# Pairs of chunks in halves, u by one product, one more chunk transposed by DMA, and another order of all steps

## The chip, the cores and the metric

The kernel runs on one core of a Trainium2 chip. The metric is the device time of one execution in microseconds. Engines, as the profile names them: PE (TensorE matmul; PEld is its weight load), DVE (VectorE), ACT (ScalarE), POOL (GpSimd) and SP (SyncE), whose queue issues nearly all DMAs here.

## The reference

Two parts, the second on the result of the first. B = 4, H = 8, S = 768, D = 48; the second part has 3072 tokens, 384 inputs and 2048 inner columns.

```python
    for t in range(S):
        kt, vt, rt, wt = (k[:, :, t].copy(), v[:, :, t].copy(), r[:, :, t].copy(), w[:, :, t].copy())
        cur = np.einsum('bhd,bhe->bhde', u[None] * kt, vt)
        y[:, :, t] = np.einsum('bhd,bhde->bhe', rt, state + cur)
        state = wt[:, :, :, None] * state + np.einsum('bhd,bhe->bhde', kt, vt)
...
    h = x @ w_in
    g = np.maximum(0.01 * h, h)
    return (g @ w_out).astype(np.float32)
```

`x` is `y` with the heads side by side, one row a token.

## The kernel before, in words

The sequence of every batch entry is cut into chunks of 128 tokens: 4 entries of 6 chunks, 24 chunks with the numbers n = 0 to 23 in the order of `seq`. For a chunk the recurrence becomes matrix products. The logarithm of w is summed over the tokens by a product with a triangular matrix (cum); exponentials of the sums scale r and k (the rk products on DVE); r and k are transposed (tr by PE and a copy, or trk/trk2 by a DMA transpose); scores are k against r, masked on DVE; intra multiplies the masked scores with v and adds what the state gives; the state goes on to the next chunk of the entry. What u adds is taken separately: ru and ruk on POOL, a sum over a head (dg) on DVE, vs on POOL. The result y of a chunk is transposed into `xT`, by PE and a copy (ty, ty_copy) or by a DMA (ty_dma, ty_dma2).

The first four chunks are two pairs (`pair`, lines 390 to 599): a pair loads 256 tokens of an entry at once, two tokens to a partition, j = 0 and 1. `PARTS` (line 64) cuts the first pair into two halves of four heads; the second runs whole. `HALVES` (line 65) names the tensors that are loaded in halves where there are parts. A part has three cum products (banks c1, c0, cg) and four exponentials, one each for k and r and for j = 0 and 1, and four rk products, four transposes and four copies. The other 20 chunks go by `single` (lines 604 to 751); `run` (753 to 788) joins the chunks in `MERGED` with the next one, and `RK_DMA` (line 61) says whose r and k a DMA transposes, `Y_DMA` whose y.

The second part works on blocks of one or two chunks (`BLOCKS`, line 69). An up step (up2 for two chunks) is six products of `w_in_b` with `xT` into one PSUM bank (line 846); ACT applies the leaky function into `g` (line 858); a down step is four products of `g` with `w_out_b` (line 871), four of them to a chunk; the result is copied into one of 24 `o` buffers (line 877) and stored (line 830). The weights come in ten pieces as float32 (line 299) and are cast to bfloat16 by DVE, ACT or POOL.

The order of all work is written out as `TABLE` (lines 73 to 123): each word is an engine's letter (P, V, A, G for POOL, S for SP) and the number of a step in the order in which `step` was called; `Z512` is a product of zeros with 512 columns, which keeps PE at work while there is nothing else. `HOMES` says which buffer of its pool each tile takes. `issue` (lines 40 to 58) calls the steps in that order, so each engine's own order is that of its words, and an engine waits at an instruction whose input is not there, with all its later ones behind it. The pools are small: 7 `in` buffers for loads, 8 PSUM banks, 24 `o` buffers. Line 231 is the helper of all element-wise products, 235, 237 and 239 the copies on POOL, DVE and ACT, 242 the helper of all products; 353 and 384 are PE's transposes.

The vector u must lie on all partitions (`ub`). Before, its one row is split into three bfloat16 parts of decreasing size by two subtractions on DVE, and three products with a single row of ones (lines 336 to 339) add them up on 128 partitions; DVE copies the sum out.

Of the kernel before, what the change touches and what calls it, by code (L numbers as in the profile page):

```python
# [8 lines left out]
BF16 = mybir.dt.bfloat16  # L9
# [15 lines left out]
class Steps:  # L25
# [51 lines left out]
P94 V72 G57 S145 P93 A102 P95 G65 V49 A99 P96 S91 P73 A101 G56 P81 A98 V75 A97 P76 A100 G154 P77 V74 P79 S151
V106 P66 S156 G121 P78 V103 P107 A82 V67 P104 G117 P83 V108 A105 P80 P68 V112 A84 V85 G155 P113 A69 V109 A114
P86 V148 A87 P110 G118 S149 A111 P740 S159 A146 G122 P129 V119 P132 V131 A741 P732 S162 G116 V134 P730 G120 A733
V123 P738 G115 A731 V130 G124 A152 P125 V133 P136 A739 V126 S165 P138 P135 S171 P137 P127 A158 V157 P736 S168  # L80
V139 A128 P742 S173 V142 A737 P140 V150 P744 A743 A141 P143 P734 A745 V144 P758 V161 G160 A735 P768 A759 P760
A769 P752 A761 V163 P746 A164 S252 P770 P762 A771 P766 V167 A763 G166 S201 P764 A175 A767 P177 P772 S172 A765
V178 P753 A179 S200 A773 P754 A180 V169 G170 P747 S231 V181 P748 A256 P183 S174 P749 V184 G216 P258 S202 V750
P755 A260 A261 V259 P774 G187 A756 S253 V182 A263 P775 A262 G188 P185 A204 S757 P780 V186 S229 V189 P206 P191
S203 V207 P776 V193 A208 G176 P777 S295 A209 V192 G190 P194 P781 A778 V211 G217 A195 V210 P196 P214 S254 P782
V197 A215 G270 V265 P198 P212 V218 S232 A199 P783 A213 P268 A233 P790 S230 V269 A784 P220 A791 G205 P235 S785
V222 P788 G219 A238 A237 S356 V236 P223 P786 A789 G297 S327 V221 G251 A224 P792 A787 V264 S292 G274 P225 A239
P266 A793 P794 V226 G234 A240 V241 P227 G271 P795 V267 S779 A228 V242 P243 S255 P804 G247 V272 A244 S324 P245
A805 P278 G248 P802 V246 S293 V279 P275 A803 G358 V249 P796 G329 V284 G250 P797 S294 V276 A296 P806 V285 A798
S353 P298 V277 A807 P800 G257 V299 S799 P280 G273 A801 P286 S326 P288 V281 A303 P808 S376 V287 A328 A302 V289  # L90
P282 P330 G310 A300 P809 V305 S355 A283 A332 V331 A301 P290 P308 G311 A291 P810 V304 A335 V309 S436 P822 G314
A334 V312 A333 P306 A357 P824 G313 S325 A823 P359 A307 G343 V336 P318 P826 S378 A362 V319 A361 A825 G375 P315
V360 A380 P811 S354 V317 A364 P382 A827 V316 P828 S377 A385 A812 V383 P820 A829 G449 P320 S419 A386 P814 A821
V321 G339 A363 P816 V337 S416 A815 V365 P347 A387 G340 P322 V388 P818 S338 A817 V348 A384 P390 A819 P367 G398
V366 P830 A368 V391 S437 G371 V341 P402 P369 P831 V389 S473 A370 G342 V403 P392 P832 V323 A393 G372 P846 S751
A420 P399 G421 V373 A847 S435 G394 P422 V408 S418 P842 A425 A424 V401 G434 P344 A843 P833 S813 V423 G374 S417
V346 P848 A427 A834 G450 V400 P844 A849 S492 V409 P404 A426 G395 P850 A845 V451 S835 V405 P836 S471 V396 A439
P406 V345 P837 A407 S491 V428 P441 P349 A443 P838 V442 S633 V350 A444 P851 A445 G453 V429 A446 P351 V447 P839
G430 S438 V352 P458 V448 P858 A840 V459 G431 S454 P862 A859 P860 A475 V432 A863 P477 G433 P856 A861 V478 S841
G504 P864 A479 S490 A857 P866 A482 G646 A865 P872 A867 G505 P870 A480 A481 S545 P873 G440 A871 V506 S379 G489  # L100
P874 V483 P466 G452 P455 S524 V467 P852 V457 S472 P853 V465 P868 A494 V464 S543 A854 P496 V456 A869 P468 P878
V497 S474 V469 A499 P460 A501 G381 P879 S470 A500 V461 G397 A498 P410 V503 P412 A528 V411 P462 P880 S544 A463
V413 G508 P530 V484 S581 P414 P875 A533 V502 G485 A415 S493 V531 P881 A876 G486 A535 P888 V882 S877 A532 A534
P884 G476 S509 V487 A889 G542 P898 A885 P513 A547 G488 P916 V514 A899 P549 G557 A917 S883 P890 V550 S526 P894
G558 A552 A553 P912 A891 V555 G495 A895 V559 P896 G507 A551 A554 P519 S525 P886 A913 G561 V556 S598 A897 P892
V520 A887 P510 S546 A893 P900 V512 P920 S599 V517 P914 V518 S601 P901 V536 A915 V511 G538 P521 S579 P902 V537
G539 V522 A602 P515 S562 P903 V516 G560 P604 V540 A904 P918 V605 G548 P906 A607 G612 A919 S523 P574 A608 P907
V575 A609 G603 P908 A606 V611 G616 P909 A583 P627 P585 V910 P921 S905 A588 V628 A587 S580 G597 P922 V586 S600
P923 A589 A590 S527 V591 P563 V924 P938 V564 S925 P934 V572 A939 S634 P936 V573 A935 S683 P926 V565 A937 G593
S855 V592 P576 A927 P940 S632 V577 G594 P928 V610 A941 S578 G613 P932 V595 A929 P930 A933 G529 V614 S617 P948  # L110
G541 A931 P566 P568 G647 V567 P942 V569 G615 P943 S911 V648 S582 P570 P944 A571 A636 P945 P638 A946 P968 V639
S947 P958 A641 A969 S651 P956 A642 S652 A959 V644 P618 S654 A957 P964 V626 A640 A643 G650 P960 V620 A965 S653
P954 G584 V645 A961 G596 V619 P962 S681 A955 V625 P621 P623 A963 V622 P976 S700 A655 V624 P629 G665 P657 S701
V630 P977 A659 A660 V658 G669 P978 S631 A662 P966 G656 A661 V664 G666 P949 V663 A967 P950 A685 S670 V667 P951
G668 A704 P687 P979 A952 V688 P706 G714 A689 S953 P970 A691 V707 S635 A980 P992 V693 A692 A711 P984 A993 V713
P986 A690 S981 A985 G699 P982 S703 A709 A987 P971 S682 A708 A983 G718 S702 P671 A710 P972 V672 P973 S684 V673
G637 P988 V676 A974 G649 P674 V677 S975 A989 P990 V675 G705 P678 A991 P996 V679 G695 P994 V694 S680 A997 P998
G696 V712 A995 P999 G715 V697 P1000 S719 P1001 G686 V716 G698 P1004 A1002 G717 P1005 S1003 P1016 P1024 A1017
P1012 A1025 P1014 A1013 P1010 A1015 P1020 A1011 P720 A1021 P1026 V721 P1018 V722 P1006 V725 A1019 P723 V726
P1027 V724 P727 P1007 V728 P1022 S729 A1008 P1028 A1023 P1032 P1033 S1009 P1034 P1035 P1029 A1036 P1046 S1037  # L120
V1030 P1050 S1031 A1047 P1040 A1051 P1042 A1041 P1044 A1043 P1038 A1045 P1048 A1039 P1052 A1049 P1060 A1053
P1054 P1055 P1056 P1057 P1061 A1058 P1062 S1059 P1063 A1064 S1065
"""
HOMES = (
    "011210004235675110025210037100001114300041341020240167253225224320212025111271366401653130562140410444310107"
    "444272305601001212120043005177140225601220401051021114200353274511022260670313331121036313301196100440121742"
    "504220870120064100260413210122710123450512147342005013010101002312517222025412461372403310044031120141615210"
    "020122604062612005060072121072217511121234633241173402213183112102134400002021020524174643000102607102234261"
    "9510011101604132200034052000102211712121223536200045025736374120325140253603166271113648046455256290a114706b"
    "0735102751c5d1336653223e4f041115g1357257360h1i0572622253k6j1016020610l4m075127623107n12604375151320"  # L130
# [4 lines left out]
def kernel(  # L135
# [58 lines left out]
    ones_f = pool.tile([1, 128], BF16, name="ones_f")  # L194
# [97 lines left out]
    def weights(which, lo, hi):  # L292
# [697 lines left out]
```

## Time and profile before

| what | before |
|---|---|
| median of 3 runs | 182.56 us |
| lowest, highest | 180.97, 182.56 us |
| the profiled execution | 181.88 us |
| its span in the profile | 180.1 us |
| PE busy, instructions | 171.3 us (95%), 1960 |
| ACT, DVE, POOL busy | 118.6, 112.2, 101.3 us |
| DMA | 34.60 MB, mean 192 GB/s |

The span goes from the first instruction of the program to the last; some 1.8 us of the execution's own time lie around it. A busy PE is not PE at its peak, since its products are pipelined and overlap: the pace is read from the starts of successive ones. The DMA share is the mean busy share of the 16 DMA engines and can exceed 1, as transfers on one engine overlap.

### The profile page before, as it was taken

The page shows a single profiled execution, that of the slowest core. Times are in us where ns is not written, and L with a number is a line of the kernel's source. Part 1 is how long each engine was busy: PE and PEld are TensorE (multiplying, and loading weights), DVE is VectorE, ACT ScalarE, POOL GpSimd, SP SyncE. Part 2 cuts the span into 40 slices and gives each one's busy share as a digit, 9 for nine tenths or more (in the row PEclk, how much of TensorE's full clock was granted, in tenths as well). Part 3 has the DMA queues.
Part 4 walks back from the last instruction along what each step waited for, and adds up shares of the span by engine and source line. Part 5 has one row for each costly group of instructions (what it writes and reads, how often), then busy time and mean ns, then how long its engine had stood idle before and what let it go on. Part 6 is the DMA issues. An engine that isn't in the chain of part 4 may idle for free.

```text
span 180.1 us, 5012 instructions
## 1 busy us (share of the span) xinstructions
PE 171.3 (95%) x1960; PEld 128.1 (71%) x1960; DVE 112.2 (62%) x230; ACT 118.6 (66%) x265; POOL 101.3 (56%) x137
## 2 busy tenths in 40 slices
PE   7978899999999999999999999989999999999992
PEld 2645688766878787778777977577786786876860
DVE  7489882459688879796398587686396384070000
ACT  3676987855966898667757954555776953722821
POOL 6799722467695858947946928567068378000000
PEclk9999999999999999999999999999999999999999
DMA  5999999799998989989999999999899998403202
GB/s 147 265 315 297 346 375 333 177 202 221 177 224 159 227 156 204 231 197 195 206 186 146 244 192 165 197 218 223 201 185 169 191 216 103 126 2 91 87 0 87
DMA packets 117129, 34.60 MB, mean 192 GB/s; under 512 B 109681, under 2 KB 116338, under 8 KB 117106
## 3 DMA queue, kind: packets, MB, share of 16 engines
q1 hardware_dynamic: 117104, 34.28, 91.6%
q8 instruction: 15, 0.25, 0.6%
q14 instruction: 8, 0.07, 0.2%
q10 hardware_dynamic: 2, 0.00, 0.0%
HBM read 25.17 MB, written 4.72 MB: 166 GB/s over the span
## 4 chain that ended last, share of the span: by engine, by line
PE 61%; DMA 12%; ACT 7%; POOL 6%; DVE 5%; issue 5%; SPq 2%; POOLq 0%; DVEq 0%; ACTq 0%
PE ps L242 59%; DMA in<-in_w_dram 6%; DMA in<-in_r_dram 3%; POOL ru L231 3%; DMA xT<-y 2%; DVE rk L231 2%; DVE m L231 2%; ACT g L858 2%; PE ps L353 1%; SPq L618 1%; ACT ps L651 1%; POOL sb L231 1%; POOL vs L231 1%; ACT lw L626 1%; POOL vb L235 1%
## 5 line engine op out<-in xcount | busy, mean ns | idle before, releaser
L242 PE MATMUL ps<-xT,w_in_b 128*128 128x256 bf16 (+1 forms) x672 | 70.6, 257 | 0.9 <-DMA xT<-y 0.6
L242 PE MATMUL ps<-w_out_b,g 128*128 128x384 bf16 x384 | 71.4, 326 | 0.0
L858 ACT ACTIVATE g<-ps 128x512 bf16<-128x512 f32 x96 | 56.4, 597 | 14.5 <-PE ps L242 12.3
L242 PEld LDWEIGHTS <-w_in_b 128*128 128x128 bf16 x672 | 57.1, 98 | 8.8 <-issue 0.8
L242 PEld LDWEIGHTS <-g 128*128 128x128 bf16 x384 | 34.7, 97 | 18.9
L231 DVE TENSOR_TENSOR m<-ps,maskb 128x512 bf16<-128x512 f32 x40 | 25.3, 683 | 9.9 <-PE ps L242 9.6
L231 DVE TENSOR_TENSOR rk<-ps,in 128x384 bf16<-128x384 f32 (+1 forms) x52 | 26.2, 520 | 7.9 <-ACT ps L651 2.6
L231 POOL TENSOR_TENSOR ru<-in,ub 128x384 f32<-128x384 f32 x24 | 23.8, 1001 | 11.5 <-DMA in<-in_k_dram 11.2
L231 POOL TENSOR_TENSOR sb<-s,a 128x384 bf16<-128x384 f32 x18 | 14.9, 830 | 17.3 <-ACT a L647 13.9
L231 POOL TENSOR_TENSOR ru<-ru,in 128x384 f32<-128x384 f32 x24 | 23.8, 1001 | 0.8
L239 ACT COPY o<-ps 128x384 f32<-128x384 f32 x19 | 9.1, 480 | 16.1 <-PE ps L242 16.0
L231 POOL TENSOR_TENSOR vs<-in,dg 128x384 f32<-128x384 f32 x20 | 16.5, 830 | 1.6 <-DVE dg L367 1.6
L235 POOL CAST vb<-in 128x384 bf16<-128x384 f32 x24 | 12.0, 504 | 8.4 <-DMA in<-in_v_dram 8.4
L367 DVE TENSOR_REDUCE dg<-ru 128x8 f32<-128x384 f32 x24 | 13.1, 547 | 5.3 <-POOL ru L231 5.1
L231 DVE TENSOR_TENSOR ci<-ps,lw 128x384 f32<-128x384 f32 x20 | 11.1, 555 | 6.6 <-PE ps L242 3.6
L231 DVE TENSOR_TENSOR y<-ps,vs 128x384 bf16<-128x384 f32 x20 | 11.1, 553 | 4.2 <-PE ps L242 4.2
L242 PEld LDWEIGHTS <-rkT 48*128 48x128 bf16 (+2 forms) x304 | 10.6, 97 | 3.5 <-issue 1.7
L626 ACT ACTIVATE lw<-in 128x384 bf16<-128x384 f32 x20 | 10.3, 521 | 3.1 <-DMA in<-in_w_dram 3.1
L647 ACT ACTIVATE a<-ps 64x4 f32<-64x4 f32 x36 | 6.1, 169 | 8.3 <-PE ps L242 4.2
L651 ACT ACTIVATE ps<-ps 128x384 f32<-128x384 f32 x20 | 9.6, 481 | 2.3 <-DVE ci L231 2.0
L654 ACT ACTIVATE ps<-ci 128x384 f32<-128x384 f32 x20 | 9.8, 496 | 0.9 <-DVE ci L231 0.9
L353 PE MATMUL ps<-ident,rk 128*128 128x128 bf16 x88 | 9.0, 227 | 1.4 <-DVE rk L231 1.2
(75 smaller groups left out, 164.3 us busy)
## 6 DMA issues: line engine op xcount, KB each, us to landing
out_dram<-o SPq DMA_DIRECT2D x24, 192.0 KB, 3.4
in<-in_r_dram SPq DMA_DIRECT2D x22, 192.0 KB, 4.3
in<-in_w_dram SPq DMA_DIRECT2D x22, 192.0 KB, 4.1
in<-in_k_dram SPq DMA_DIRECT2D x22, 192.0 KB, 4.3
in<-in_v_dram SPq DMA_DIRECT2D x20, 192.0 KB, 4.3
in<-in_moe_w_out_dram SPq DMA_DIRECT2D x4, 768.0 KB, 10.4
in<-in_moe_w_in_dram SPq DMA_DIRECT2D x2, 768.0 KB, 7.0
in<-in_moe_w_in_dram SPq DMA_DIRECT2D x4, 384.0 KB, 7.5
```

Of the source, the lines that this page charges most:

```text
L231: (nc.gpsimd if e == "POOL" else nc.vector).tensor_tensor(out=o, in0=a, in1=b, op=op)
L235: nc.gpsimd.tensor_copy(out=o, in_=i)
L239: nc.scalar.copy(out=o, in_=i)
L242: nc.tensor.matmul(o, lhsT=a, rhs=b, start=start, stop=stop, skip_group_check=True)
L353: nc.tensor.transpose(view()[:, g - g0, :], rk.t[:, kind, 2 * g : 2 * g + 2, :].rearrange("p h d -> p (h d)"), ident[:])
L367: "dg", "DVE", lambda e: nc.vector.tensor_reduce(out=dg.t[:], in_=ru.t[:], axis=AX.X, op=ALU.add),
L618: lambda e, src=src, i=i: nc.sync.dma_start(out=part(i)(), in_=src[b, :, t0 : t0 + L, :].rearrange("h p d -> p h d")),
L626: "ln", "ACT", lambda e: nc.scalar.activation(out=lw.t[:, :, 0:D], in_=wv(), func=AF.Ln),
L647: lambda e, q0=q0: nc.scalar.activation(out=a_in.t[q0 : q0 + 64, :, q0 // 64], in_=cp.t[q0 : q0 + 64, DM : DM + NP], func=AF.Exp),
L651: "er", "ACT", lambda e: nc.scalar.activation(out=heads(cp.t), in_=heads(cp.t), func=AF.Exp),
L654: "ek", "ACT", lambda e: nc.scalar.activation(out=heads(ek.t), in_=ci.t[:], func=AF.Exp, scale=-1.0),
L858: lambda e, hp=hp, g=g, j=j, J=J, N=N: nc.scalar.activation(out=g.t[:, j : j + J, 0:N], in_=hp.t[:, 0 : J * N].rearrange("p (a n) -> p a n ...
```

## The change

1. Both pairs now run in two halves of four heads. For each half, one bank holds k of both tokens (j = 0 and 1, 2 x 192 columns) and another r of both; each is made of four cum products of 192 columns. One exponential then takes a whole bank of 384 columns, one rk product both tokens, one transpose step four 128 x 128 pieces and one copy 512 columns. A pair has four of each where the first pair had eight and the second four.
2. Loads: the first pair's w, k and r come in halves as before, the second pair's w now too.
3. u: the three parts are written to rows 0, 32 and 64 of a zeroed 128-row bfloat16 tile, and one product with a 128 x 128 matrix of ones replaces the three. There are four DVE instructions (two subtractions, two copies) and a zeroing for the two subtractions.
4. `RK_DMA` has 10 in the place of 9. Chunk 10 is merged with 11, so one DMA transposes r and k of the 11th and 12th chunk; those of the 10th go to PE and two copies.
5. The cast of v (vb) may run on ACT; 15 of the 24 do.
6. `TABLE` and `HOMES` are new throughout, and so are the step numbers. Columns of zeros rise from 4320 to 6784. SP's first loads are now a half of k, of r, of k, then the two halves of w, r and v; before, r, w, k, w, k, r, v. The ten weight pieces all come ahead of the first load of a single chunk. Two w_in casts run on ACT and six on POOL (before three on DVE, three on ACT, two on POOL). No store is issued until 21 up and 29 down steps are left; then 20 of the 24 come between and behind the last loads and transposes, in an order of their own.

The first words of the new table, its first up step (P720), the place where the first stores stand, and its end:

```diff
-RK_DMA = {9, 12, 13, 14, 16, 17, 18, 19, 20, 22}
+RK_DMA = {10, 12, 13, 14, 16, 17, 18, 19, 20, 22}
...
-PARTS = {0: [(0, 2), (2, 4)]}
-HALVES = 'wkr'
+HALVES = {0: 'wkr', 2: 'w'}
...
+A0 S12 P1052 S13 A1 S11 S9 V2 S10 V4 S14 V3 S15 V5 V6 S139 Z512 Z512 Z512 Z512 Z512 Z512 Z512 Z512 Z256 Z256 P7
+S73 A8 S74 G47 S75 A16 Z512 Z512 Z512 Z224 P18 G43 A17 P19 S76 A25 P21 G48 A29 P20 V26 A37 V30 Z256 Z160 P22 A33
...
+V111 A98 G108 P720 V119 A102 P113 G112 V118 A721 P124 P120 V114 S143 P123 A148 G147 P128 V121 P127 S149 P115
...
+V698 A975 G655 P673 S737 P982 S821 A676 V674 G682 S785 P962 A983 P978 A678 G672 V683 A677 G701 P963 V680 A675
+A979 V679 P970 S939 G685 V702 S705 P964 A971 G684 P959 G691 P657 A960 P965 S869 V659 S891 P980 V658 A966 S827
+P984 V663 A981 P660 V662 P976 V661 S911 P664 S771 G703 A977 P985 S765 V665 S961 P990 S666 P706 P991 V707 P986
+V712 S897 S863 P992 V708 S933 P987 V711 S841 S967 P709 A988 S799 P713 S743 P993 V710 S989 P1006 V714 A994 P1002
+S715 A1007 P1004 A1003 P996 A1005 S995 P998 A997 P1000 A999 P1008 A1001 P1010 A1009 P1018 A1011 P1028 P1036
...
+P1047 V1022 P1048 S1023 P1012 P1049 P1013 A1050 P1014 S1051 P1040 P1015 P1041 V1016 P1042 S1017 P1043 A1044
+S1045
```

In it S737, S821, S785, S939, S869 and so on are stores; S705 and S715 are the DMA transposes of the last two chunks' r and k and of their y, S666 that of chunks 20 and 21; P1028 is the first up step of the last block. P741, a little behind the first up steps, is the last down step of block 0.

```diff
+    s_u = step("u_mm", "PE",
+               lambda e: mm(u_ps.t[:, 0:DM], ones_b[:], u_top.t[:].rearrange("p h d -> p (h d)"), True, True),
+               deps=[s_u0, s_u2, s_u3], reads=[u_top], takes=[u_ps])
...
-        return vb, step("vb", "POOL", lambda e: copy(e, vb.t[:], vv()), at, deps=vl, reads=slots, takes=[vb])
+        return vb, step("vb", "POOL ACT", lambda e: copy(e, vb.t[:], vv()), at, deps=vl, reads=slots, takes=[vb])
...
             def go(e):
-                for j in range(2):
-                    mm(heads(bank.t)[:, 2 * g0 : 2 * g1, :], mats[j][:], lw.t[:, j, 2 * g0 : 2 * g1, 0:D], j == 0, j == 1)
-            return step("cum2" + half, "PE", go, n, deps=[s_lns[x]], reads=[lw], takes=[bank])
+                for q in range(2):
+                    mm(quantities(bank.t)[:, q], both[:], lw.t[:, j2, h0:h1, 0:D], q == 0, False)
+                for q in range(2):
+                    mm(quantities(bank.t)[:, q], mats[q][:], lw.t[:, 1 - j2, h0:h1, 0:D], False, True)
+            return step("cum2_h", "PE", go, n, deps=[s_lns[x]], reads=[lw], takes=[bank])
...
+            kb, rb = Bf("ps", "cp2"), Bf("ps", "cp2")
+            banks.append((kb, rb, cum(x, kb, tstr2, 0, (tinc2, tstr2)), cum(x, rb, tinc2, 1, (tinc2, tstr2))))
...
+            for a, bank, s_c, scale in ((1, kb, s_kb, -1.0), (0, rb, s_rb, 1.0)):
...
+                s_e = step(
+                    "exp2", "ACT",
+                    lambda e, bank=bank, scale=scale: nc.scalar.activation(
+                        out=bank.t[:, 0 : 2 * HW], in_=bank.t[:, 0 : 2 * HW], func=AF.Exp, scale=scale),
+                    n, deps=[s_c], reads=[bank])
```

More of the change, by code (lines that the diff above doesn't have):

```diff
@@ L77 @@
[L77 to L81, printed above, removed]
@@ new lines, in tcopy @@
+                def tcopy(e, tiles=tiles, a=a, g0=g0, g1=g1):
+                    if a:
+                        o = rkT()[:, NP + g0 : NP + g1, :].rearrange("p g (j t) -> p j g t", j=2)
+                    else:
+                        o = rkT()[:, g0:g1, :].rearrange("p g (t j) -> p j g t", j=2)
+                    copy(e, o, tiles())
+                s_tr = step("tr", "PE", tpose, n, deps=[s_d], reads=[rkw], takes=[tr])
+                s_T[x].append(step("tr_copy", "DVE ACT", tcopy, n, deps=[s_tr], reads=[tr], takes=[rkTb]))
```

196 lines of the change are left out of this document (91 added, 105 removed).

## The prediction, made before the result

> **What bounds the kernel now.** I read the table of windows first, cut where the work changes; then PE's and DVE's timelines; then the waits.
>
> The windows (span, busy us and instructions of each engine, PE clock, DMA share, GB/s):
>
> ```profile
> 0.00:18.84 18.84, 15.15 (x176) 8.72 (x176) 14.57 (x46) 11.97 (x31) 15.46 (x32) 1.00 1.01 259
> 18.84:38.70 19.86, 19.33 (x234) 15.07 (x234) 11.63 (x22) 15.56 (x29) 7.83 (x9) 1.00 1.01 294
> 38.70:126.10 87.40, 86.38 (x1070) 67.00 (x1069) 66.37 (x129) 61.42 (x144) 62.49 (x77) 1.00 1.06 198
> 126.10:176.60 50.50, 50.46 (x485) 37.33 (x482) 19.66 (x35) 29.18 (x62) 15.48 (x20) 1.00 0.68 126
> ```
>
> From 18.84 us, where the first up product starts, to 176.6 us PE is busy 156.2 of 157.8 us. DMA share is about 1 until 126 us, but in that time PE lacks only 1.55 us. So PE bounds everything behind 18.84 us. PE's timeline shows that it is also dense inside:
>
> ```profile
> 26.62 2.79 PE L242 MATMUL ps<-xT,w_in_b 128*128 128x256 bf16 x24
> 29.25 1.46 PE L242 MATMUL ps<-w_out_b,g 128*128 128x384 bf16 x8
> 30.55 2.78 PE L242 MATMUL ps<-xT,w_in_b 128*128 128x256 bf16 x24
> 36.88 0.39 PE L353 MATMUL ps<-ident,rk 128*128 128x128 bf16 x4
> 37.10 0.81 PE L242 MATMUL ps<-w_out_b,g 128*128 128x384 bf16 x4
> ```
>
> The starts give the pace: (29.25 - 26.62)/24 = 0.110 us an up matmul, (30.55 - 29.25)/8 = 0.163 us a down matmul, (37.10 - 36.88)/4 = 0.055 us a transpose. An up step is 6 matmuls, 0.66 us; a down step 4, 0.65 us. The time can therefore change in four places only: how soon PE is full, how much PE has to do, PE's remaining waits, and the tail behind the last matmul, one copy from 176.60 to 177.08 and one store up to 180.1, the same in both kernels:
>
> ```profile
> 176.60 0.48 ACT o L239
> ```
>
> **The front.** Here PE has gaps, because the first four chunks (two pairs) pass through ACT, DVE and PE by turns. What counts is how much of the later work is done at a given time. By 38.67 us before has done:
>
> ```profile
> 18.00:38.67 20.67, 11.64 (x96) 9.16 (x96) 2.59 (x3) 2.49 (x3) 0.00 (x0) 1.00 1.01 295
> 18.00:38.67 20.67, 5.69 (x33) 2.24 (x4) 0.83 (x1) 3.58 (x3) 1.00 1.01 295
> ```
>
> The first row is the instructions that touch w_in_b: 96 matmuls, 16 up steps. The second is those of w_out_b: 32 matmuls done and one under way, 8 down steps. Beside these lie two cum steps and one transpose step of later chunks. In the new order the same 16 up and 8 down steps, with one cum step, end with the step P741; it lacks a cum of one matmul of 384 and four small ones (0.27 us) and a transpose step (0.22 us), 0.49 us in all. When does it get there?
>
> Loads. In the new order w's first half is the fourth DMA, not the second. The four loads have the same size and the queue is in order, so I take the times of the places:
>
> ```profile
> 1.32 0.49 SPq L400 DMA_DIRECT2D in<-in_w_dram  x1
> 2.40 0.51 SPq L400 DMA_DIRECT2D in<-in_w_dram  x1
> 4.25 0.53 ACT L417 ACTIVATE lw<-in 128x384 bf16<-128x384 f32 x1 [1.62 <-DMA in<-in_w_dram]
> in<-in_w_dram SPq DMA_DIRECT2D x1, 192.0 KB, 4.1
> ```
>
> The fourth place is issued at 2.40 and lands 4.1 us later, at 6.5 us; the second place let the logarithm start at 4.25. So the chain starts 2.25 us later. k and r are there by then, where before they came last: its first rk product waits until 7.36.
>
> ```profile
> 5.77 0.69 PE L242 MATMUL ps<-lw,tstr 128*128 128x192 bf16 x3
> 6.25 0.37 PE L242 MATMUL ps<-lw,tinc 128*128 128x192 bf16 x1
> 7.36 1.59 DVE L231 TENSOR_TENSOR rk<-ps,in 128x192 bf16<-128x192 f32 x5 [1.33 <-ACT ps L456]
> 14.93 1.02 DVE L231 TENSOR_TENSOR rk<-ps,in 128x384 bf16<-128x384 f32 x2
> 15.87 0.55 DVE L231 TENSOR_TENSOR sb<-ps,a 128x384 bf16<-128x384 f32 x1
> 16.34 0.41 DVE L237 COPY rkT<-ps 128x512 bf16<-128x512 bf16 x1
> 16.67 0.55 DVE L231 TENSOR_TENSOR rk<-ps,in 128x384 bf16<-128x384 f32 x1
> 21.79 1.28 DVE L231 TENSOR_TENSOR m<-ps,mask 128x512 bf16<-128x512 f32 x2
> ```
>
> At this point a cum matmul of 192 takes (6.25 - 5.77)/3 = 0.16 us. New chain: landing 6.5, logarithm 0.53, the warm-up matmuls ahead of cum end near 7.3, four cum matmuls 0.64, 0.2 until the last is done (0.37 in its row less its pace of 0.16), an exp of 384:
>
> ```profile
> L456 ACT ACTIVATE ps<-ps 128x384 f32<-128x384 f32 x4 | 1.8, 475 | 0.7 <-PE ps L242 0.6
> L367 DVE TENSOR_REDUCE dg<-ru 128x8 f32<-128x384 f32 x24 | 13.1, 547 | 5.3 <-POOL ru L231 5.1
> ```
>
> DVE's first rk product comes at about 8.7 us, 1.3 us later than 7.36.
>
> From there DVE carries the chain. An instruction behind another one starts some 0.08 us sooner than durations say: two rk products fill 14.93 to 15.87, 0.47 each, sb takes 0.47 until the next, a copy 0.33; two masks end 1.28 after the first's start, 0.6 apart. I take the same off dg (0.547) and the xT copy (0.36). Up to the fourth chunk's xT the new order has 31 DVE instructions: 8 rk products at 0.47, 4 dg at 0.46, 3 rkT copies at 0.33, 8 masks at 0.61, 2 sb, 2 y and one keep (casts and copies of the same 384) at 0.47, 3 xT copies at 0.28. That is 3.8 + 1.8 + 1.0 + 4.9 + 2.3 + 0.8 = 14.6 us. Before runs more in that place:
>
> ```profile
> 7.30:18.80 11.50, 10.45 (x26) 1.00 1.14 301
> 18.80:27.20 8.40, 7.26 (x13) 1.00 1.07 366
> 26.80 0.36 DVE L237 COPY xT<-ps 128x384 bf16<-128x384 bf16 x1 [0.24 <-PE ps L384]
> ```
>
> 39 DVE instructions, 17.7 us busy, end at 27.16: the smaller pair-0 forms are joined two to one, and the three w_in casts go to ACT and POOL. With 1.5 us for waits between engines the new chain gives the fourth xT at 8.7 + 14.6 + 1.5 = 24.8 us. The first 20 of the 31 (9.5 us, 0.4 of waits) give the first up at 18.6, as before; five up steps of block 0 then lie between the second pair's pieces. From 24.8 us: 11 up steps 7.2, 8 down steps 5.2, cum 0.2, so P741 ends at 37.4 against 38.67.
>
> Bounds: if DVE followed by its durations (31 times some 0.08 us more), 2.5 us are lost and the front is 1.2 us worse; if the matmuls run at full rate sooner, another 0.2 better, -1.5. I take -0.8, as my chain leaves out hand-offs that only a run shows.
>
> The 0.16 us a matmul of 192 halves only at about 9.2 us (9.27 0.33 below). [...]
>
> ```profile
> 9.27 0.33 PE L242 MATMUL ps<-lw,tstr 128*128 128x192 bf16 x2
> 9.50 0.29 PE L353 MATMUL ps<-ident,rk 128*128 128x128 bf16 x2
> ```
>
> Edits that end in this front and are priced with it: u's three one-row products become one, with four DVE pieces and a zeroing ahead of it (about 2 us of DVE from 3.4, done near 5.5, ahead of w's landing; no cover needed beyond that). Cum grows from 2304 to 3072 columns a pair, 0.33 us a pair, in PE's gaps. 2464 more warm-up columns run while nothing else can.
>
> **PE's work.** r and k of chunk 9 go to TensorE (+8 transposes), those of 10 and 11 to one DMA (-16): 8 less, 8 x 0.055 = 0.44 us, and two rkT copies less. This and the lacking 0.49 us cancel, so both kernels have the same work left at the two times compared; it is not counted again. The DMA transposes grow by one chunk, 0.26 MB, while 24 stores leave that stretch.
>
> **PE's waits behind the front.** Those that a transfer made:
>
> ```profile
> 49.55 0.56 DVE L231 TENSOR_TENSOR rk<-ps,in 128x384 bf16<-128x384 f32 x1 [0.55 <-DMA in<-in_r_dram]
> 50.17 0.40 PE L353 MATMUL ps<-ident,rk 128*128 128x128 bf16 x4 [0.34 <-DVE rk L231]
> 117.67 1.59 PE L242 MATMUL ps<-xT,w_in_b 128*128 128x256 bf16 x13 [0.59 <-DMA xT<-y]
> ```
>
> The new order puts no store on SP's queue before PE has 35 us left, so loads and transposes no longer stand behind 20 of them. Bounds: none goes, or all that PE lacks behind 38.7 us in the windows above, 1.02 + 0.04 = 1.06 us. I take -0.6, the two rows' 0.93 less a new small wait. What is late next: the first loads of single chunks now start behind all weights (near 31 us of data), against 21.6; before's queue has a hole at 34 to 36 us, and 8 down steps of block 1 (5.2 us) cover chunk 4's chain. I take 0 for that.
>
> 15 of the 24 v casts move from POOL to ACT (7 us), which also copies out g for PE:
>
> ```profile
> L235 POOL CAST vb<-in 128x384 bf16<-128x384 f32 x24 | 12.0, 504 | 8.4 <-DMA in<-in_v_dram 8.4
> L858 ACT ACTIVATE g<-ps 128x512 bf16<-128x512 f32 x96 | 56.4, 597 | 14.5 <-PE ps L242 12.3
> ```
>
> POOL waited 8.4 us for v. On ACT a late v holds the g behind it, and PE once the banks are full. Bounds 0 and 15/24 of 8.4, 5.3 us. Loads are less crowded and a g waits for PE 12.3 us in all, so near 0: +0.2.
>
> **The tail.** 20 of the 24 stores and the last transposes now share 20 us. Between the issue of the transpose of chunks 20, 21 and that of the last xT stand two rk transposes (0.52 MB each), 19 stores and two xT transposes (0.2 MB each), 5.2 MB. PE has 15 up and 15 down steps (19.7 us) and about 3 us of scores, intra and cum from the first to the product that needs the last, 22.6 us.
>
> ```profile
> 162.20:164.00 1.80, 1.80 (x13) 1.08 (x11) 0.00 (x0) 0.60 (x1) 0.00 (x0) 1.00 0.58 114
> 166.50:168.50 2.00, 2.00 (x21) 1.79 (x19) 0.22 (x1) 1.57 (x3) 0.00 (x0) 1.00 0.54 197
> xT<-y SPq DMA_TRANSPOSE x6, 3.5
> ```
>
> The first window holds one xT transpose: 1.04 us of DMA for 0.2 MB. The second holds two stores: 0.54 us each. So 2 x 2.7 + 19 x 0.54 + 2 x 1.04 = 17.7 us; with 3.5 to land 21.2 of 22.6. It fits, narrowly. Bounds: 0, or at the 198 GB/s of the middle window 26 + 3.5 - 22.6 = 7 us. Nearest are the windows without loads: +0.4.
>
> **Sum.** -0.8 - 0.6 + 0.2 + 0.4 = -0.8 on 181.88 us, the profiled execution (span 180.1): 181.1 us. That execution lies 0.7 below the median of 182.56; the runs span 180.97 to 182.56.
>
> **Rivals.** Stores as a wall (slower): the last xT transpose stands behind eight stores, the first up of the last block waits. For it: 21.2 of 22.6 us. Against it: stores alone move 0.39 MB in 1.08 us of DMA, 365 GB/s. It decides once the 5.2 MB move below some 5.2/(22.6 - 3.5) = 270 GB/s; at 220 it costs 4.5 us in place of 0.4, 185.2. [...]
>
> The front doesn't come earlier: DVE's hand-offs cost what its durations say, +1.2 in place of -0.8, 183.1. For it: w 2.25 us later. Against it: the starts quoted.
>
> The whole gain: front -1.3, 1.06 us of waits gone, tail free: 179.5. For it: the sum of DVE's work; against it: every new order has waits of its own.
>
> v casts hold ACT: 3.5 us of the 5.3 reach PE, 184.4 and up; against it ACT's share of 66%:
>
> ```profile
> PE 171.3 (95%) x1960; PEld 128.1 (71%) x1960; DVE 112.2 (62%) x230; ACT 118.6 (66%) x265; POOL 101.3 (56%) x137
> ```
>
> **How the numbers follow.** Within 1% is about what a measurement of this kernel can tell from no change: 180.7 to 184.4 about the median. Forecast 0.45, the whole gain 0.22, the front lost 0.17, stores 0.11, v casts 0.05. The range takes the whole gain, with 0.3 for the sooner full rate, and the front lost, and ends where the store case begins: 179.2 to 184.4. Faster: the whole gain and a quarter of the forecast, 0.33. Slower: stores, v casts and a little of the front lost, 0.19. The rest, 0.48, is within 1%.
>
> **What would show it.** Right: DVE's first rk near 8.7 us, the first up near 18.6, the fourth xT near 25, P741's down near 37.5; no PE wait over 0.3 us from 40 to 140; the last xT transpose landing ahead of its up. Wrong: the fourth xT behind 27, ACT waiting for v over 1 us with PE waiting for a bank, a PE gap near 160 us that ends with the xT transpose.

## The result and the profile after

The changed kernel runs in 180.37 us (median of 18 runs, 179.44 to 181.11) beside 182.17 us for the kernel before (18 runs, 180.97 to 183.25): ratio 0.9897, 95% interval 0.9879 to 0.9915, about 1.9 us. The profiled execution took 180.32 us with a span of 178.6 us; before it was 181.88 and 180.1.

The table of windows of the changed kernel, cut where the first up starts, where the front ends and at the same 38.7 and 126.1 us as before (length, then busy us and instructions of PE, PEld, DVE, ACT and POOL, clock, DMA share, GB/s):

```profile
0.00:19.27 19.27, 15.74 (x209) 9.90 (x209) 14.69 (x43) 12.57 (x29) 15.27 (x31) 1.00 0.95 243
19.27:37.40 18.13, 18.13 (x206) 14.11 (x207) 7.55 (x16) 14.19 (x25) 7.36 (x9) 1.00 1.03 317
38.70:126.10 87.40, 87.05 (x1093) 67.50 (x1091) 68.95 (x135) 67.59 (x162) 58.07 (x70) 1.00 1.10 183
126.10:174.70 48.60, 48.59 (x458) 36.18 (x455) 18.69 (x35) 25.41 (x53) 13.18 (x17) 1.00 0.76 164
```

PE lacks, in what follows, what its busy time is short of a window. It lacked 0.53 us between the first up and 38.7 us before and lacks nothing now up to 37.4; between 38.7 and 126.1 us it lacked 1.02 us and now 0.35; in the last stretch at most 0.04 in either kernel. ACT has 6.2 us more and POOL 4.4 less in the third row, in the main the v casts.

PE's and DVE's timeline, the lines that answer to those of the prediction:

```profile
7.53 0.33 PE L241 MATMUL ps<-lw,tstr 128*128 128x192 bf16 x2 [0.20 <-ACT lw L417]
7.70 0.24 PE L241 MATMUL ps<-lw,tinc 128*128 128x192 bf16 x1
8.63 1.02 DVE L230 TENSOR_TENSOR rk<-ps,in 128x384 bf16<-128x384 f32 x2 [3.07 <-ACT ps L469]
19.27 0.83 PE L241 MATMUL ps<-xT,w_in_b 128*128 128x256 bf16 x6 [0.28 <-DVE xT L236]
24.51 8.07 PE L241 MATMUL ps<-xT,w_in_b 128*128 128x256 bf16 x72
24.55 0.62 DVE L236 COPY xT<-ps 128x384 bf16<-128x384 bf16 x2 [0.56 <-PE ps L383]
36.97 0.33 PE L241 MATMUL ps<-lw,trev 128*128 128x384 bf16 x1
37.13 1.14 PE L241 MATMUL ps<-w_out_b,g 128*128 128x384 bf16 x6
```

| | before | after | predicted |
|---|---|---|---|
| DVE's first rk product | 7.36 | 8.63 | 8.7 |
| first up | 18.84 | 19.27 | 18.6 |
| fourth xT done | 27.16 | 25.17 | 24.8 |
| 16 up and 8 down steps done (P741) | 38.67 | 37.8 | 37.4 |
| last matmul ends | 176.6 | 174.7 | |
| span | 180.1 | 178.6 | |

P741 is the first four of the six matmuls at 37.13: 37.13 + 4 x 0.163 = 37.8. So 0.9 us is won in the front and 1.0 us between its end and the last matmul; 0.4 us of it is given back after the last matmul (3.9 us to the end of the span instead of 3.5). The last store takes 1.9 us from issue to landing in both; the 0.4 us lie behind its landing (1.5 us to the end of the span instead of 1.1). All three traces with the old end have 3.5 us there, ten of the eleven with the new end 3.8 to 3.9 and one, e7, 3.5. No run looked for the cause.

How firm is the front's 0.9? Six traces below and here have the changed front untouched. Their first up starts at 18.63 to 19.27 us and P741's last matmul, the 32nd of the down matmuls, at 36.98 to 37.62, on average 37.35. Three traces with the old front have their 32nd at 37.97 to 38.51, on average 38.29. The front is worth 0.9 us either way; the first up itself doesn't come sooner, and one trace can't place it to better than 0.6 us.

### The profile page after: what moved, and what is told of

Same layout as the page of the kernel before. It is cut to its first block, busy times and chain, and to the rows that moved or that the text cites. A ratio compares the mean times of both kernels' runs of the same rounds, so it can differ in the third digit from the quotient of the medians.

```text
span 178.6 us, 5041 instructions
## 1 busy us (share of the span) xinstructions
PE 170.8 (96%) x1969; PEld 128.5 (72%) x1969; DVE 111.1 (62%) x228; ACT 121.3 (68%) x270; POOL 95.1 (53%) x124
## 3 DMA queue, kind: packets, MB, share of 16 engines
HBM read 25.17 MB, written 4.72 MB: 167 GB/s over the span
## 4 chain that ended last, share of the span: by engine, by line
PE 88%; DMA 3%; DVE 2%; ACT 2%; SPq 2%; issue 1%; DVEq 0%; ACTq 0%
PE ps L241 85%; DMA in<-in_v_dram 3%; SPq L399 2%; PE ps L352 2%; PE ps L383 1%; ACT rkT L238 1%; DVE rk L230 1%; PE ps L488 1%; ACT ps L469 0%; DVE dg L366 0%; ACT o L238 0%; DVE m L230 0%; DVE y L230 0%; DVE rkT L236 0%; ACT a L453 0%
## 5 line engine op out<-in xcount | busy, mean ns | idle before, releaser
L241 PE MATMUL ps<-xT,w_in_b 128*128 128x256 bf16 (+1 forms) x672 | 69.9, 257 | 0.3 <-DVE xT L236 0.3
L241 PEld LDWEIGHTS <-g 128*128 128x128 bf16 x384 | 35.2, 97 | 19.3
L230 DVE TENSOR_TENSOR rk<-ps,in 128x384 bf16<-128x384 f32 x48 | 25.6, 551 | 8.3 <-ACT ps L469 3.4
L238 ACT COPY o<-ps 128x384 f32<-128x384 f32 x15 | 7.2, 479 | 20.4 <-PE ps L241 20.2
L236 DVE COPY o<-ps 128x384 f32<-128x384 f32 x9 | 5.0, 554 | 18.2 <-PE ps L241 18.1
L238 ACT COPY rkT<-ps 128x512 bf16<-128x512 bf16 x14 | 8.6, 622 | 2.3 <-PE ps L352 1.2
L241 PE MATMUL ps<-rkT 48*128 48x128 bf16 (+1 forms) x224 | 8.2, 218 | 1.4 <-ACT a L453 1.2
```

The lines of the kernel that those rows point to most:

```text
L230: (nc.gpsimd if e == "POOL" else nc.vector).tensor_tensor(out=o, in0=a, in1=b, op=op)
L236: nc.vector.tensor_copy(out=o, in_=i)
L238: nc.scalar.copy(out=o, in_=i)
L241: nc.tensor.matmul(o, lhsT=a, rhs=b, start=start, stop=stop, skip_group_check=True)
```

## Experiments

Twelve kernels, each timed in five rounds against the kernel before on its own chip, so the ratios compare; the changed kernel's is 0.9897 on this scale, and 0.001 is 0.18 us.

### Late stores

**e1: early stores in the changed kernel.** The words of the stores are moved; two of the twenty:

```diff
-V661 S911 P664 S771 G703 A977 P985
+S243 V187 P763 S771 A227 A228 V226
...
-P980 V658 A966 S827 P984 V663 A981
+V415 G475 P398 S827 V464 P392 P444
```

> The changed kernel with only its stores moved: the stores of chunks 0 to 19 stand as far behind their copies as in the kernel before (1 to 34 us of PE work), not in PE's last 35 us. Theory A (late stores are what took PE's transfer waits away behind the front): 0.6 to 1.0 us of the gain goes, 181.0 to 181.4 us, and PE shows waits of 0.3 us or more behind rk transposes and loads between 40 and 130 us. Rival B (the waits went for other reasons, the stores are hidden wherever they stand): 180.1 to 180.6, no new wait.

187.15 us, ratio 1.0255 (1.0206 to 1.0304): 3.6% over the changed kernel, some 6.5 us where theory A gave at most 1.0. PE's row from 40 to 130 us, and one place of its timeline:

```profile
40.00:130.00 90.00, 86.44 (x1067) 66.09 (x1066) 66.89 (x130) 66.99 (x159) 55.60 (x65) 1.00 1.05 198
```

```profile
82.47 1.04 SPq L841 DMA_DIRECT2D out_dram<-o  x1
87.16 0.59 SPq L841 DMA_DIRECT2D out_dram<-o  x1
92.19 1.32 SPq L629 DMA_DIRECT2D in<-in_r_dram  x1
93.56 0.70 SPq L629 DMA_DIRECT2D in<-in_v_dram  x1
97.95 0.56 DVE L227 TENSOR_TENSOR rk<-ps,in 128x384 bf16<-128x384 f32 x1 [1.15 <-DMA in<-in_r_dram]
98.61 0.51 ACT L235 CAST vb<-in 128x384 bf16<-128x384 f32 x1 [1.06 <-DMA in<-in_v_dram]
99.17 0.33 PE L238 MATMUL ps<-vb,rk 128*128 128x96 bf16 x4 [0.84 <-ACT vb L235]
```

PE lacks 3.56 us where the changed kernel lacks 0.35. Two of the moved stores stand on SP's queue ahead of the loads of r and v, and take 1.6 us to issue; the loads are issued at 92.19 and 93.56 and need 5.7 and 5.0 us to land, DVE and ACT wait 1.1 us, and PE waits 0.84 us for ACT's cast. From the first up to the last matmul the trace has 161.3 us against 155.4, so most of the loss lies there, in part in waits that busy time hides. Rival B falls, and so does the size in theory A: the changed order leaves its loads too little lead for stores in these places.

**e2: late stores in the kernel before.** Chunks 0 to 19, for instance

```diff
-A791 G205 P235 S785 V222 P788 G219
+G696 V712 A995 P999 S785 G715 V697 P1000 S779 S975 S719
```

> The kernel before with only its stores moved: chunks 0 to 19 are stored where PE has as much work left as in the changed kernel (35 to 14 us), the last four as they were. Theory A (late stores take transfer waits away): 0.6 to 1.0 us faster than before, 181.2 to 181.6 us, the 0.34 and 0.59 us waits gone. Rival B (stores hidden): 182.0 to 182.4. Rival C (the stores stand as a wall ahead of the last transposes): 183 us and more, with a PE gap behind 150 us.

182.49 us, ratio 0.9998 (0.9970 to 1.0026): nothing gained. But the windows show two changes that cancel. First the kernel before, then e2:

```profile
40.00:130.00 90.00, 88.98 (x1108) 69.19 (x1106) 66.35 (x129) 63.24 (x150) 61.30 (x76) 1.00 1.05 198
130.00:165.00 35.00, 35.00 (x360) 26.05 (x355) 18.15 (x33) 20.48 (x45) 15.48 (x20) 1.00 0.84 142
```

```profile
40.00:130.00 90.00, 89.96 (x1121) 70.26 (x1119) 67.75 (x132) 64.34 (x153) 62.04 (x78) 1.00 0.99 172
130.00:165.00 35.00, 33.88 (x343) 25.00 (x342) 16.66 (x31) 18.91 (x41) 14.59 (x20) 1.00 0.93 210
```

What PE lacks from 40 to 130 us falls from 1.02 to 0.04 us, as theory A has it; from 130 to 165 us it rises from 0 to 1.12, as rival C has it. The place, in the timeline of e2:

```profile
148.48 2.05 SPq L828 DMA_DIRECT2D out_dram<-o  x4
150.64 3.22 SPq L761 DMA_TRANSPOSE rkT<-rk  x1
153.91 3.54 SPq L828 DMA_DIRECT2D out_dram<-o  x7
156.52 0.62 PE L240 MATMUL ps<-rkT 48*128 48x128 bf16 x16 [1.12 <-DMA rkT<-rk]
```

The last rk transpose is issued behind these four stores and three more just ahead of them, at 150.64 us where the kernel before had it at 149.76, though PE is sooner here; PE stands 1.12 us before the scores that need it.

**e2b: the same with seven stores behind that transpose.**

```diff
-P990 S883 S905 V675 G705 P678 S841
...
-P999 S785 G715 V697 P1000 S779 S975 S719 P1001
+P1000 S719 S883 S905 S841 S925 S785 S779 S975 P1001
```

> The kernel before with late stores as in the run e2, but the 7 stores that stood there ahead of the rk transpose of chunks 22, 23 (of chunks 10, 11, 7, 13, 3, 2, 16) now stand behind it. Theory A2 (late stores do save waits from 30 to 130 us, about 1.2 us by e2's trace, and e2 lost it again in one PE wait of 1.1 us at 156 us, where scores waited for that transpose): 1.0 to 1.3 us below before, ratio 0.993 to 0.995, no PE wait over 0.3 us at 156. Rival B (the stores are worth nothing, e2's wait at 156 would be replaced by another): ratio 0.998 to 1.002.

181.01 us, ratio 0.9929 (0.9895 to 0.9962).

```profile
40.00:130.00 90.00, 89.93 (x1116) 70.17 (x1115) 67.56 (x132) 63.94 (x152) 61.91 (x78) 1.00 0.99 171
130.00:165.00 35.00, 35.00 (x352) 25.85 (x350) 17.00 (x31) 19.29 (x42) 14.48 (x19) 1.00 0.95 210
```

The wait is gone and PE lacks 0.07 us in both rows together. Theory A2 holds: late stores alone are worth 0.7% (0.4 to 1.0) if that transpose doesn't stand behind the seven; fifteen stores ahead of the last xT transpose, at 160.00, cost PE nothing. So the stores alone, moved in the old order, win some two thirds of what the whole change wins (1.0%). The changed order has its last rk transpose ahead of all but four of the late stores.

### Transposes by DMA or by TensorE

**e6: the pair 10, 11 on TensorE again** (the headline of the change undone).

```diff
-RK_DMA = {10, 12, 13, 14, 16, 17, 18, 19, 20, 22}
+RK_DMA = {12, 13, 14, 16, 17, 18, 19, 20, 22}
```

> The changed kernel with r and k of chunks 10 and 11 (the 11th and 12th) transposed by TensorE instead of by one DMA: 16 transposes of 0.055 us and four rkT copies more (two on DVE, two on ACT), one DMA transpose of 0.52 MB less, four PSUM banks used in their free time. Theory P (PE's work is the bound there): 16 x 0.055 = 0.88 us slower than the changed kernel, ratio 0.994 to 0.996. Rival D (the DMA is what runs short in the middle; e3 and e3b, with one more DMA transpose, lost 0.6 to 1 per cent): the freed 0.52 MB takes waits of PE away, ratio 0.988 to 0.991. Rival E (the copies hold DVE and ACT): above 0.997.

181.36 us, ratio 0.9981 (0.9945 to 1.0017): 0.8% above the changed kernel where 16 x 0.055 us gives 0.5%. From the first up to the last matmul the traces have 156.5 us against 155.4: 1.1 us, of which theory P's transposes are 0.88, and one wait of PE for ACT's logarithm, 0.3 us, is new. So theory P holds for most of it in the trace; the ratio itself lies in rival E's range, above 0.997, and its interval can't tell the two apart. Rival D falls: taking 0.52 MB from the DMA frees nothing that PE waits for.

**e3: chunk 9 by DMA as well.**

```diff
-RK_DMA = {10, 12, 13, 14, 16, 17, 18, 19, 20, 22}
+RK_DMA = {9, 10, 12, 13, 14, 16, 17, 18, 19, 20, 22}
```

> The changed kernel with chunk 9's r and k transposed by a DMA too: 8 transposes of 0.055 us and two rkT copies fewer, one DMA transpose of 0.26 MB more; scores of chunk 9 moved behind the fourth next PE step so that the DMA has 5 us, three PSUM banks renamed. Theory P (PE's work is the bound, each transpose removed is 0.055 us): 0.44 us faster, 179.8 to 180.1 us. Rival D (the DMA is as loaded there, its share is over 1, so the transpose or the loads behind it are late): no gain or a loss, 180.4 to 181.2, with a PE wait at scores, intra or a load behind 65 us.

182.25 us, ratio 1.0002 (0.9967 to 1.0037): not 0.44 us faster but 1.9 slower than the changed kernel.

```profile
62.74 1.01 DVE L227 TENSOR_TENSOR rk<-ps,in 128x384 bf16<-128x384 f32 x2
64.69 2.04 SPq L691 DMA_TRANSPOSE rkT<-rk  x1
66.80 1.19 SPq L629 DMA_DIRECT2D in<-in_v_dram  x2
70.39 0.51 ACT L235 CAST vb<-in 128x384 bf16<-128x384 f32 x1 [1.69 <-DMA in<-in_v_dram]
70.95 0.33 PE L238 MATMUL ps<-vb,rk 128*128 128x96 bf16 x4 [0.87 <-ACT vb L235]
```

Chunk 9's rk products end at 63.75, so the transpose does not wait for DVE, as theory Q below supposes; its issue alone holds SP's queue for 2.04 us. Chunk 9's load of v stands behind it, ACT waits 1.69 us for v and PE 0.87 us for ACT. The scores, at 68.75, wait for nothing.

**e3b: that load ahead of the transpose.**

```diff
-A347 S344 V327 S328 A810 G377 V369 P349 A802 S317
+A347 S344 V327 S317 S328 A810 G377 V369 P349 A802
```

> As e3 (chunk 9's r and k by a DMA as well), with the load of chunk 9's v put ahead of the new transpose on SP's queue, not behind it. Theory Q (e3 lost its gain because the queue is in order: the transpose waited for DVE and v of chunk 9 stood behind it, ACT's cast came 1.7 us late and PE waited 0.9 us at sums): that wait goes, ratio 0.987 to 0.990, at or below the changed kernel's 0.990. Rival D (the transposes and loads are short of DMA there): the waits at 70 us stay in another place, ratio 0.995 and more.

181.60 us, ratio 0.9959 (0.9939 to 0.9979), 1.1 us above the changed kernel.

```profile
63.03 1.01 DVE L227 TENSOR_TENSOR rk<-ps,in 128x384 bf16<-128x384 f32 x2
65.30 1.26 SPq L629 DMA_DIRECT2D in<-in_v_dram  x1
66.67 1.67 SPq L691 DMA_TRANSPOSE rkT<-rk  x1
70.40 0.40 PE L238 MATMUL ps<-rkT 48*128 48x128 bf16 x8 [1.22 <-DMA rkT<-rk]
```

The wait for v goes and another comes: scores now wait 1.22 us for the transpose, which needs 3.7 us from its issue. Rival D has the sign; theory Q was right that v had stood behind the transpose. Without that wait the scores would start 5.1 us behind the chunk's rk products, which end at 64.04; the load of v takes the queue until 66.56 of it. In e3 the transpose came in time and v didn't, here it is the other way round: the lead is enough for one of them and not for both. In the changed kernel the pair 10, 11 has 7.7 us between its last rk product and its scores. Whether another order would give chunk 9 that lead wasn't tried.

### The casts of v

**e7: twelve v casts back on POOL**, as in

```diff
-A287
+G287
```

> The changed kernel with the 12 v casts of single chunks (6 to 11, 13, 14, 17, 18, 20, 21 of those on ACT) back on POOL, same places. The prediction charged the move to ACT with 0.2 us. Theory V (ACT holds g, PE waits for a bank): 0.2 us faster or more, 179.8 to 180.2. Rival W (POOL was what got late: a late v holds ru, sb and vs behind it there): 0.3 to 1.0 us slower, 180.7 to 181.4, with PE waits at intra or sums. Rival X: no difference, 180.2 to 180.6.

181.15 us, ratio 0.9929 (0.9897 to 0.9961), 0.6 us above the changed kernel (-0.1 to 1.3).

```profile
40.00:130.00 90.00, 88.67 (x1109) 68.26 (x1107) 70.15 (x136) 62.67 (x149) 64.73 (x82) 1.00 1.09 176
```

```profile
53.22 0.99 POOL L227 TENSOR_TENSOR ru<-ru,in 128x384 f32<-128x384 f32 x1
54.18 0.99 POOL L227 TENSOR_TENSOR ru<-in,ub 128x384 f32<-128x384 f32 x1
55.12 0.49 POOL L231 CAST vb<-in 128x384 bf16<-128x384 f32 x1
55.67 0.33 PE L238 MATMUL ps<-vb,rk 128*128 128x96 bf16 x4 [0.44 <-POOL vb L231]
```

PE lacks 1.33 us instead of 0.35 from 40 to 130 us. The cast doesn't wait for v: it stands behind two ru products of 1 us on POOL, and PE waits for it. From the first up to the last matmul the trace has 157.1 us against 155.4. That is rival W by another road than it named; the time alone leaves it within reach of no difference, the trace doesn't.

### The front

**e4: three w_in casts on DVE.**

```diff
-G140 ... G138 ... G142
+V140 ... V138 ... V142
```

> The changed kernel with three of the w_in casts of its front on DVE again, as in the kernel before (there 0.69 to 0.95 us each), in their places of the order: one ahead of the first pair's masks, two behind the second pair's. Theory F3 (the prediction's: the front ends where DVE's instructions end, so what was taken off DVE is the front's gain): the first up 0.6 to 0.9 us later, the fourth xT 1.8 to 2.5 us later, the end of the front (16 up and 8 down steps) 0.8 to 2 us later than the changed kernels' 37.0 to 37.6, ratio 0.994 to 1.001. Rival L3 (loads and POOL set it): end of the front within 0.4 us, ratio 0.988 to 0.992.

182.01 us, ratio 1.0027 (0.9999 to 1.0054), 1.3% above the changed kernel.

```profile
22.48 0.95 DVE L233 CAST w_in_b<-in 128x768 bf16<-128x768 f32 x1
24.26 0.95 DVE L233 CAST w_in_b<-in 128x768 bf16<-128x768 f32 x1
25.12 0.55 DVE L233 CAST y<-ps 128x384 bf16<-128x384 f32 x1
25.73 0.51 PE L380 MATMUL ps<-ident,y 128*128 128x128 bf16 x6 [1.36 <-DVE y L233]
```

The two casts stand ahead of y on DVE, PE waits 1.36 us for it, and P741's last matmul starts at 39.19 instead of 37.35. Theory F3 holds for the end of the front: what DVE does ahead of the fourth xT adds to its length. Its first up, 0.6 to 0.9 us later, doesn't come: it lies at 19.31, beside 18.63 to 19.27. The casts alone cost more here than the whole front gained, so the run shows that they matter, and leaves open what the joined halves are worth.

**e5: w's first half first**, with the second group of zeros moved back.

```diff
-A0 S12 P1052 S13 A1 S11 S9 V2 S10
+A0 S9 S12 P1052 S13 A1 S11 V2 S10
...
-A16 Z512 Z512 Z512 Z224 P18 G43 A17 P19 S76 A25 P21 G48 A29 P20
+A16 A8 S74 G47 S75 P18 G43 A17 P19 S76 A25 P21 G48 A29 P20 Z512 Z512 Z512 Z224
```

> The changed kernel with w's first half as the first load, the logarithm of it ahead of the copy of u, and the second group of warm-up matmuls (1760 columns) behind the first four cum steps. Theory F (the prediction's: DVE carries the front from its first rk product on, so the chain moves with it): first rk product near 7.1 us instead of 8.6, first up 1.0 to 1.5 us sooner, 0.5 to 1.2 us faster than the changed kernel, ratio 0.983 to 0.987. Rival L (the front hangs on other loads too: ACT's v cast, which waits for v until 9.8 us, and POOL's ru products, which pace dg): first rk sooner, first up within 0.3 us of 18.6 to 19.3, ratio 0.988 to 0.992.

180.47 us, ratio 0.9911 (0.9875 to 0.9946). It tells nothing of the chain: the first rk product came at 8.51 us, as its exp stood on ACT behind the logarithm of w's second half.

**e5b: the same, with the engines' orders fitted to it.** The words of ACT, of DVE and of PE without its zeros:

```diff
-A8 A16 A17 A25 A29 A37 A33 A42 A24 A32 A23 A41
+A16 A8 A25 A29 A17 A37 A33 A32 A24 A42 A23 A41
...
-V26 V30 V49 V28 V34 V38 V45 V56
+V26 V30 V28 V34 V38 V56 V49 V45
...
-P7 P18 P19 P21 P20 P22 P27 P1053 P31 P55
+P7 P18 P19 P27 P21 P31 P20 P22 P1053 P55
```

> The run e5 again, now so that the engines can use the early w: e5's first rk product did not come sooner (8.5 us), since on ACT the first exps stood behind the logarithm of w's second half, which landed at 7.6. Here ACT takes both exps of the first half ahead of that logarithm and the rkT copy ahead of the v casts, PE transposes the first rk products ahead of the second half's cum, DVE takes both dg behind the first mask, and 992 warm-up columns are left out. Theory F (the front moves with DVE's first rk product and its order): first rk at 6.9 to 7.3 us, first up 0.8 to 1.4 us sooner than the changed kernels' 18.6 to 19.3, ratio 0.981 to 0.986. Rival L (v's landing at 9.8 us and POOL's ru products hold the chain): first rk at 7.1, first up 18.4 to 19.2, ratio 0.988 to 0.992.

180.67 us, ratio 0.9915 (0.9885 to 0.9946).

```profile
6.87 1.02 DVE L227 TENSOR_TENSOR rk<-ps,in 128x384 bf16<-128x384 f32 x2 [1.30 <-ACT ps L466]
9.63 1.02 DVE L227 TENSOR_TENSOR rk<-ps,in 128x384 bf16<-128x384 f32 x2 [1.28 <-ACT ps L466]
11.60 0.66 PE L238 MATMUL ps<-vb,rk 64*128 64x96 bf16 x12 [0.55 <-ACT vb L235]
```

The first rk product is 1.8 us sooner, and the first up (19.94 us) is not. The next two rk products wait 1.28 us for the exps of w's second half, the state's sums wait for the cast of v: rival L, but by w's second half too, which it didn't name.

**e9: pair 0 ahead of pair 2.** PE's and DVE's words around the first up:

```diff
-P39 P81 P80 P61 P53 P65 P58 P66 P62 P89 P83 P84 P82 P63 P64 P93 P101 P71 P97 P68 P117 P720
+P39 P81 P80 P58 P61 P53 P65 P66 P62 P83 P63 P64 P84 P82 P89 P93 P71 P68 P101 P720 P97 P117
...
-V52 V36 V57 V88 V59 V60 V92 V100 V96 V94 V107 V72 V111
+V52 V36 V57 V59 V60 V88 V92 V90 V100 V72 V96 V107 V111
```

> The changed kernel with the pieces of the first two pairs in another order: pair 0's second scores, masks, intra, y copies and xT ahead of pair 2's rk products and transposes, the first up right behind them, one keep and one y copy of pair 2 on ACT instead of DVE, one w_in cast earlier on POOL. Same steps, no work added or removed. Theory F2 (what counts is real work done on PE before the first up and how soon that comes; DVE's order sets it): first up 1.0 to 1.5 us sooner, 0.4 to 0.9 us faster than the changed kernel, ratio 0.984 to 0.988. Rival L2 (between 19 and 25 us PE then runs out of work, since w_in's casts and pair 2's chain come no sooner): first up sooner, but PE waits 0.5 us and more from 19 to 25 us, ratio 0.989 to 0.992.

181.87 us, ratio 0.9959 (0.9929 to 0.9989). The first up comes at 18.08 us, some 0.9 sooner, and P741's last matmul at 40.92, 3.6 later. The row of PEclk (forty slices of 4.5 us), and the timeline:

```profile
PEclk9999969999999999999999999999999999999998
```

```profile
20.11 0.83 POOL L231 CAST w_in_b<-in 128x768 bf16<-128x768 f32 x1 [1.77 <-DMA in<-in_moe_w_in_dram]
21.78 0.34 PE L238 MATMUL ps<-y,spread 64*128 64x384 bf16 x2 [0.49 <-POOL y L227]
22.57 0.34 PE L238 MATMUL ps<-y,spread 64*128 64x384 bf16 x2 [0.45 <-POOL y L227]
23.42 1.49 PE L238 MATMUL ps<-xT,w_in_b 128*128 128x256 bf16 x6
25.27 1.98 PE L238 MATMUL ps<-xT,w_in_b 128*128 128x256 bf16 x12
```

I had put one w_in cast ahead on POOL, where it waits 1.77 us for its load. The vs products behind it are late, PE waits twice for them, and then six up matmuls take 1.49 us where they take 0.83 at 19.27 in the changed kernel: 0.213 us from start to start instead of 0.109. Rival L2, and half the pace on top. This execution took 183.26 us, 1.4 above the run's median, so the half pace need not be in every execution.

**e10: that cast back behind the vs products.**

```diff
-A79 G147 S141 P66
+P113 G112 G147 V118
```

> The run e9 with one step put back: POOL's w_in cast behind both vs products of pair 2 again. In e9 that cast waited 1.8 us for its load, the vs products behind it came late, PE waited 0.5 us twice, and its matmuls then ran at half pace from 22.8 to 26.3 us. Theory G (that cast alone cost e9 its gain, through PE's waits and the half pace): no up matmul at 0.213 us, PE lacks less than 1.5 us from 20 to 30 us where e9 lacked 4.1, ratio 0.985 to 0.990. Rival H (the new order of the pieces itself leaves PE without work behind the first up): up matmuls at half pace again or waits over 0.3 us from 19 to 25 us, ratio 0.993 and more.

180.48 us, ratio 0.9927 (0.9905 to 0.9949).

```profile
21.86 0.82 PE L238 MATMUL ps<-xT,w_in_b 128*128 128x256 bf16 x6
```

No matmul at half pace; PE lacks 1.3 us from 20 to 30 us instead of 4.1 (starts beyond the usual pace). The mechanism of theory G holds. Its gain doesn't come: with the first up at 18.06, P741's last matmul starts at 38.06, 0.7 behind the changed kernels. The first up sooner is worth nothing if DVE's later pieces are not sooner too.

No run beat the changed kernel; e5 and e5b are the nearest, and their intervals hold 0.9897.

## Why the prediction was right, and where it was not

The time and the sign came out: 181.1 us forecast, 180.37 measured, in the range. The size did less well: 0.8 us forecast, 1.5 in the span of the profiles and 1.9 by the ratio, and 180.37 lies just outside the band within 1% (from 180.7) that got the largest chance. By its steps:

- **The front, -0.8: right, measured -0.9 in the profile and between the means of the traces.** The first rk product (8.63 for 8.7), the fourth xT (25.17 for 24.8) and P741 (37.8 for 37.4) lie near where the sum of DVE's instructions put them. For the first of them that is in part luck: w's half lands at 6.9 us and not at 6.5, the cum steps start at 7.53 and not at 7.3, and they make it good with 0.083 us a matmul in place of 0.16. The 0.2 us that the bounds give a sooner full rate, 0.3 in the range, is an estimate of the author's that no run shows as a term of its own; what the runs showed is this pace of the first four cum matmuls, which makes them 0.3 us shorter than at 0.16. The chain itself gave -1.3, and the allowance for hand-offs made it -0.8. e4 shows a part of the cause: casts given back to DVE cost 1.3%. The joined halves were not tried alone. One sentence of the step fails: that DVE carries the chain "from there", its first rk product. e5b moves that product by 1.8 us and nothing follows. By e5b's waits the chain is DVE's from the middle of the first pair on; ahead of that it hangs on w's second half and v.
- **PE's transfer waits, -0.6: right.** PE lacks 0.67 us less between 38.7 and 126.1 us. e2 and e2b show that the stores were the cause, worth 0.95 us of PE's waits; the changed order has 0.3 us of new ones, as the step allowed.
- **v casts on ACT, +0.2: not there.** ACT's casts wait 0.2 us in all in the changed kernel (the groups: busy us, mean ns, idle us ahead of them), and PE waits for none of them.

```profile
L238 ACT CAST vb<-in 128x384 bf16<-128x384 f32 x15 | 7.6, 518 | 0.2
L234 POOL CAST vb<-in 128x384 bf16<-128x384 f32 x9 | 4.5, 505 | 0.0
```

  The term looked only at ACT's queue, where a late v would hold g, and so had no gain in its bounds. It left out the queue that the casts left: in e7 they stand on POOL behind ru products of 1 us, and PE waits 1.0 us more, 0.6 us in time (-0.1 to 1.3). That is their worth in the new order; in the old one, with all casts on POOL, PE waited for one of them, 0.4 us in the front, and for none behind it, so no run shows what the move was worth on the kernel before.
- **The tail with its stores, +0.4: the wrong place, and the size by luck.** From the issue of the rk transpose of chunks 20, 21 at 136.39 us to the landing of the last xT (issued at 155.33, 3.1 us) it took 22.0 us where the sum had 21.2 of 22.6, and PE misses nothing from 126.1 us on: the term's own cost is nothing. The 0.4 us come behind the last matmul, in the part that the prediction held to be the same in both kernels. The wall that the rival described can happen, though: e2 has it with 1.12 us, ahead of a transpose of rk and not of xT.
- **PE's work, 0.44 against 0.49, cancelled: not contradicted.** e6 gives 0.8% (0.4 to 1.2) where its 0.88 us of transposes are 0.5%; the balance itself was not measured.

So 0.9 of the gain is the front and 1.0 lies behind it, less 0.4 at the end: 1.5 us of span where the prediction had 0.8. Of the 1.0, PE's waits are 0.7; the other 0.3 no row places. The prediction was too small by these 0.3, by the 0.2 for the v casts, and by 0.1 or so in each of the front and the waits.

## What to carry to other kernels

SP's queue issued in the order of its words: in e3 a load of v stood behind the 2.04 us that a transpose took to issue. Put last on such a queue what nobody waits for, and then look at what is next behind it: late stores gave 0.7% or nothing, according to one transpose that stood behind seven of them, for which PE waited 1.12 us. When an instruction moves to another engine, price the queue that it leaves as well as the one that it joins: with the v casts back on POOL (e7) PE waited 1.0 us more. An engine order that is dense holds only with the lead of its loads, so a step put ahead "because it is ready" must be ready on every queue that it stands on: the w_in cast put ahead in e9 waited 1.77 us for its load, and PE 0.49 and 0.45 us for what stood behind it.

## What the hardware showed that was not expected

PE's pace halved for 3.5 us in one trace, behind two waits of PE. In e9 the starts of successive matmuls of 256 columns are 0.213 us apart from 23.42 to 26.31 and 0.109 behind that; smaller matmuls are slowed from 22.84 on (four of 96 columns take 0.47 us there, and 0.34 in e10), so the state lasts 3.5 us. Just ahead of it PE had waited 0.49 and 0.45 us for POOL's y; e10, whose trace has no wait ahead of the same two matmuls (21.26), kept its pace, 0.82 us for six up matmuls. In e9 PEclk has a 6 in that slice. This is one execution, and no run shows what sets the pace.

At the start the moment at which PE's pace doubles (a matmul of 192 columns takes 0.16 us from start to start ahead of it and 0.083 behind it) differs from execution to execution. The starts of the first matmuls show it at 7.0 us in the changed kernel's trace and at 4.3 to 7.1 us in eight others whose start is the same; with the old start at 5.2 us in e2, at 9.2 in the trace that the prediction had and at 9.5 in e2b. So the 9.2 was one draw, not a property of the kernel before.
